# Attention and two MoE layers on one core: TensorE transposes 8 of 18 probability blocks for two of four batches, and the first MoE's small column chain is rewritten

## The chip, the cores and the metric

The kernel runs on one core of a Trainium2 chip. The metric is the device time of one execution in microseconds (us), lower is better. The median of three runs is 1086.21 us (1083.95 to 1088.44). In what follows PE is the matrix engine (TensorE), PEld its weight loads, DVE the VectorE, ACT the ScalarE, POOL the GpSimd engine, and SP the engine whose queue issues nearly all DMA transfers.

## What is computed

```python
def _attn_ref(q, k, v, w1, b1, w2):                 # 4 batches, 8 heads, 576 positions, 64 wide
    scores = scale * np.matmul(q, k.transpose(0, 1, 3, 2)) + bias   # bias from a small MLP of i, j
    attn = np.exp(scores - max) ; attn = attn / (sum(attn) + 1e-9)
    return np.matmul(attn, v)

def _moe_ref(x, w_in, w_out, g_ln):                 # 2304 tokens, 512 -> 1024 -> 512
    h = x @ w_in
    sm = softmax(h) ; solu = h * sm
    ln = (solu - mean(solu)) / np.sqrt(var(solu) + 1e-06) * g_ln
    return ln @ w_out

def _moe2_ref(x, w_gate, w_val, w_out):             # 512 -> 1536 -> 512
    return (sigmoid(x @ w_gate) * (x @ w_val)) @ w_out
```

The attention's output, laid out as 2304 tokens of 512 numbers, goes through the first MoE and then through the second.

## The kernel before

Matrix products are done in f16 with every operand split into a high and a low part: hi is the rounded value, lo the rounded remainder, and a product takes hi x hi, hi x lo and lo x hi.

**Attention** runs as 72 ticks, numbered 0 to 71 here. A tick handles one pair of heads, one batch and 128 queries (for the last 64 positions of a sequence: 64 queries of each of two batches). Ticks 0 to 35 belong to batches 0 and 1, ticks 36 to 71 to batches 2 and 3. In tick t the program writes `a_qk(t)` (scores on PE into the PSUM tiles `s_ps`), `a_soft(t)` (DVE adds the bias and takes the maximum, L550; ACT makes the exponentials, L555 and L557), `a_split(t-1)`, `a_x(t-5)`, some side work, and `a_pv(t-4)` (L590: probabilities times values, into `xps`).

`a_split` makes the f16 parts of the probabilities: hi on ACT (L568) or, in every fourth tick, on DVE (L566); lo on POOL, 1024 columns in L569 and 128 columns in L570. All of it lies in one tile `p16` of 128 x 2304 f16, which is 18 blocks of 128 x 128. One DMA (L572, on SP's queue) transposes all 18 blocks into the tile `pt`, whose blocks are the stationary operands of `a_pv`. The DMA waits for L570, which POOL runs behind L569.

**Side work** is a list of steps, of which five (later three) are taken in each tick: tables for the attention's bias (masks on DVE at L392 and L400, matmuls on PE at L443, sums on DVE at L459 and L463, stores to DRAM as `bias_d`), then decoding and scaling of the first MoE's weights (`w1_steps`, L171 to L180 and L665 to L683), then the first MoE itself (`moe_items`). `scales` in `w1_steps` turns sums of squares into a power of two: a reduction on DVE (L145), one matmul with ones on PE (L147, tile `tot`), and a chain of small DVE operations (L152 to L160, then L689 to L693). `W1S` says how many weight blocks are decoded between the last block of a matrix and its scale.

**The first MoE** takes 18 tiles of 128 tokens. Per tile: `m_g1` (L732, `hps`), `m_ew1` and `m_ew2` (softmax times h and layer norm over 1024 columns, with a chain of operations on 128 x 1 columns of a tile `mm` at L751 to L767, one of them a power on POOL at L765), `m_ew3` (PE transposes the f32 result through the identity `id_sb`, L777 into `ltp`; ACT and DVE copy it out) and `m_g2` (L791, `x2ps`).

**What sets the order.** A scheduler orders the instructions of each engine from priorities and its own estimate of times; each engine then runs its list strictly in that order. From the point where the bias tables are done ("open", about tick 19), PE alone keeps the order in which the code is written. PSUM has two buffers for `s_ps`, one for `xps`, and a ring of three, `ps_m`, that all other PE outputs share: bias matmuls, the transposed q and k (`qtp` L279, `ktp` L240), `xtp`, `hps`, `ltp`, `x2ps`. The ring of `p16` has two buffers and later three, that of `pt` three and later four.

**After attention** the second MoE's weights are decoded and summed (DVE at L172 to L176 and L1188, POOL at L665 and L669) while the first MoE's last tiles finish, and from about 795 us to the end the second MoE's matmuls run on PE.

## Time and profile before

| | us |
|---|---|
| median of three runs | 1086.21 |
| the profiled execution | 1086.11 |
| its span, from the first instruction to the last | 1084.3 |
| 75 to 246 us: attention ticks 0 to 18 with bias tables and the first MoE's weights | 171 |
| 246 to 390 us: ticks 19 to 39 in part, first MoE begins, PE in written order | 144 |
| 390 to 575 us: the other ticks with the first MoE | 185 |
| 575 to 795 us: end of the first MoE, the second MoE's weights | 220 |
| 795 us to the end: second MoE | 289 |

The stretches are set by the starts of ticks: the last PE work of the scheduler's own order stands at about 246 us, the first tick of batches 2 and 3 at 372 us, and the last tick's scores at 563 us. PE is busy for 909.7 us of the span, DVE 776.7, ACT 620.1, POOL 411.1; busy shares are an average over stages with different limits, so the views below are read stage by stage. A wait is shown with the engine that waited, then an arrow, then what ended the wait.

### The profile page before, as it was taken

The numbers are of one execution on the slowest core, as the hardware profiler recorded it, in microseconds if no ns is written. First come the engines' busy times: TensorE is split into PE (matmuls) and PEld (weight loads), VectorE is DVE, ScalarE is ACT, GpSimd is POOL, SyncE is SP. The second block draws the span as 40 slices with busy tenths as digits, with TensorE's granted clock in tenths as the row PEclk, the third lists the DMA queues.
The fourth block names the chain that finished last, engine by engine and source line by source line (L and its number), as shares of the span: only waits on it lengthen the run. The fifth ranks groups of instructions, "written<-read, shape, count | busy, mean of one in ns | idle before, by whom it ended". The sixth has DMA issues, their size and how long they took to land.

```text
span 1084.3 us, 24456 instructions
## 1 busy us (share of the span) xinstructions
PE 909.7 (84%) x9806; PEld 650.8 (60%) x9806; DVE 776.7 (72%) x1605; ACT 620.1 (57%) x1283; POOL 411.1 (38%) x370
## 2 busy tenths in 40 slices
PE   3647584768788889989999788796999999999998
PEld 3534454545565667667776466344577866865873
DVE  6879898985566676666764989999973862881760
ACT  4787676756576788877883677754342331331331
POOL 2357455663555565545561376749000000000000
PEclk9656665779898899999999899998999999999999
DMA  7968999799789899999965536511001010001001
GB/s 229 289 212 217 228 243 266 150 215 225 158 163 188 180 196 189 188 197 204 188 115 165 171 111 193 181 41 39 35 11 54 1 52 27 1 1 39 2 1 39
DMA packets 261442, 146.58 MB, mean 135 GB/s; under 512 B 217680, under 2 KB 231504, under 8 KB 261328
## 3 DMA queue, kind: packets, MB, share of 16 engines
q1 hardware_dynamic: 259264, 143.18, 56.0%
q0 software_dynamic: 1536, 1.58, 0.5%
q8 instruction: 77, 1.26, 0.5%
q14 instruction: 37, 0.30, 0.1%
q10 hardware_dynamic: 528, 0.26, 0.1%
HBM read 82.46 MB, written 20.05 MB: 95 GB/s over the span
## 4 chain that ended last, share of the span: by engine, by line
PE 30%; DVE 14%; DMA 2%; issue 2%; ACT 2%; SPq 0%; POOL 0%; DVEq 0%; ACTq 0%
PE prod L1264 15%; PE ops L1332 10%; DVE fs L1188 4%; DVE w2f L173 2%; DVE w2f L176 2%; PE x2ps L791 2%; PE s_ps L1302 1%; DVE w2s L1188 1%; DVE gv L1170 1%; DMA wraw<-in_moe_w_val_dram 1%; PE hps L732 1%; DVE w2f L172 1%; DMA wraw<-in_moe_w_gate_dram 1%; DVE fr L1308 1%; PE xps L590 1%
## 5 line engine op out<-in xcount | busy, mean ns | idle before, releaser
L569 POOL TENSOR_TENSOR p<-p,p 128x1024 f16<-128x1024 f32 x72 | 155.4, 2159 | 152.1 <-ACT p L568 117.0
L1188 DVE TENSOR_TENSOR fr<-prod,fr 128x512 f32<-128x512 f32 x126 | 85.0, 687 | 93.9 <-PE prod L1264 92.2
L1332 PE MATMUL ops<-w2f,gv 128*128 128x512 f16 x648 | 143.3, 380 | 0.7 <-POOL w2f L669 0.7
L557 ACT ACTIVATE p<-p,m,sc 128x576 f32<-128x576 f32 x144 | 124.0, 862 | 2.8
L550 DVE CUSTOM_DVE_ANT_0 p<-s_ps,gk 128x576 f32<-128x576 f32 x144 | 104.2, 750 | 21.9 <-PE s_ps L530 17.7
L791 PE MATMUL x2ps<-lt,w1f 128*128 128x128 f16 x1728 | 108.0, 223 | 13.6 <-DVE lt L780 12.8
L791 PEld LDWEIGHTS <-w1f 128*128 128x128 f16 x1728 | 102.0, 100 | 22.9 <-issue 18.2
L1302 PE MATMUL s_ps<-xb,w2f 128*128 128x512 f16 (+1 forms) x576 | 101.8, 335 | 16.5 <-DVE fr L1308 13.6
L590 PE MATMUL xps<-gk,pt 128*128 128x64 f16 (+1 forms) x2240 | 90.1, 205 | 29.7 <-DMA pt<-p 25.3
L590 PEld LDWEIGHTS <-pt 128*128 128x128 f16 (+1 forms) x2240 | 84.6, 108 | 40.5 <-DMA pt<-p 27.2
L1332 PEld LDWEIGHTS <-gv 128*128 128x128 f16 x648 | 63.6, 98 | 74.7 <-issue 1.8
L530 PE MATMUL s_ps<-gk,qt 64*128 64x288 f16 (+1 forms) x960 | 93.9, 320 | 10.5 <-DVE m L550 5.3
L443 PEld LDWEIGHTS <-mask 128*128 128x128 f16 (+1 forms) x1312 | 62.6, 119 | 52.6 <-issue 20.7
L1302 PEld LDWEIGHTS <-w2f 128*128 128x128 f16 x576 | 57.6, 100 | 59.2 <-issue 21.5
L1264 PEld LDWEIGHTS <-w2f 128*128 128x128 f16 x864 | 84.5, 98 | 11.8 <-issue 1.1
L1169 ACT ACTIVATE gv<-fr 128x512 f16<-128x512 f32 (+1 forms) x60 | 34.9, 585 | 82.7 <-DVE fr L1322 70.4
L732 PE MATMUL hps<-w1f,xt 128*128 128x512 f16 x312 | 75.7, 392 | 0.6 <-DVE qt L282 0.6
L555 ACT ACTIVATE m<-m,sc 128x1 f32<-128x1 f32 x144 | 40.4, 286 | 54.5 <-DVE m L550 54.5
L443 PE MATMUL bp<-rhs,mask 128*128 128x64 f16 (+1 forms) x960 | 52.2, 222 | 19.8 <-DVE gb L463 12.2
L1264 PEld LDWEIGHTS <-w2s 128*128 128x128 f16 x648 | 63.4, 98 | 7.3
L530 PEld LDWEIGHTS <-qt 64*128 64x128 f16 (+1 forms) x960 | 46.8, 105 | 33.3 <-issue 12.4
L568 ACT ACTIVATE p<-p 128x1152 f16<-128x1152 f32 x54 | 62.6, 1158 | 7.0 <-DMA pt<-p 5.4
(194 smaller groups left out, 1773.3 us busy)
## 6 DMA issues: line engine op xcount, KB each, us to landing
gk<-bias_d SPq DMA_DIRECT2D x24, 576.0 KB
wraw<-in_moe_w_out_dram SPq DMA_DIRECT2D x20, 512.0 KB
wraw<-in_moe_w_gate_dram SPq DMA_DIRECT2D x12, 512.0 KB
wraw<-in_moe_w_val_dram SPq DMA_DIRECT2D x12, 512.0 KB
sraw<-in_q_dram SPq DMA_DIRECT2D x12, 384.0 KB
sraw<-in_k_dram SPq DMA_DIRECT2D x12, 384.0 KB
sraw<-in_v_dram SPq DMA_DIRECT2D x12, 384.0 KB
bias_d<-gk SPq DMA_DIRECT2D x8, 576.0 KB
```

The source lines that it names most:

```text
L443: pe.matmul(big[0:np_, jj // 8, o:o + 64], lhsT, rhs[i].rearrange("p c h g -> p (c h g)"), start=(i == 0), stop=(i == 1),)
L530: pe.matmul(ss[hh][p0:p1, n, 0:288], qt[rows, nr * ql + r, p0:p1], kt[rows, o:o + 288], start=(m == 0), stop=(m == 2))
L550: dve.tensor_tensor_reduce(out=pp[:, hh].rearrange("p (i j) -> p i j", i=2), in0=ss[hh][:, :, 0:288], in1=bi.rearrange("p (i j) -> p i j", ...
L557: act.activation(out=pp[:, hh], in_=pp[:, hh], func=ACTF.Exp, bias=m[:, 2 + hh:3 + hh], scale=col(C), accum_out=sm[:, c + hh:c + hh + 1])
L569: pool.tensor_tensor(out=p16[:, :, 640:1152], in0=pp[:, :, 0:512], in1=hi[:, :, 0:512], op=ALU.subtract)
L590: pe.matmul(o, a, b_, start=(n == 0), stop=(n == len(seq) - 1))
L732: pe.matmul(h, xt[:, xl, kk, off:off + 128], win16[:, 2 * kk + n, wl], start=(kk == 0 and xl == 0 and wl == 0), stop=(kk == 3 and xl == 1),)
L791: pe.matmul(ps[:, dc], wout16[:, f, wl, 128 * dc:128 * dc + 128], lt[:, ll, f], start=(n == 0), stop=(n == 23))
L1188: dve.tensor_tensor(out=out_, in0=a, in1=b, op=op)
L1264: pe.matmul(p[:, jf, 0:nn], w(wl, kk, jf), x(xl, kk), start=(m == 0), stop=(m == 5))
L1302: pe.matmul(ps[:, 0:n], w[:, 4 * (j // 4) + c, wl, o:o + 128], xx[:, 0:n, c, xl, :], start=(m == 0), stop=(m == 11))
L1332: pe.matmul(ps, gvs[j // 4][:, gl, j % 4, 128 * tt:128 * tt + 128], w2h16[2][:, j, wl], start=(m == 0), stop=(m == 35))
```

## The change

For ticks of batches 0 and 1 (`on_pe`), the DMA transposes only the first 10 of the 18 blocks (hi and the 64-column remainders); the other 8 blocks (lo, 512 columns for each of two heads) are transposed by PE against an f16 identity `id16` into a `ps_m` tile `plo`, and ACT copies that tile into the last 8 blocks of `pt` (`a_lo`, written one tick after the split). For this `p16` and `pt` are laid out with the 10 blocks first, POOL does the 128-column operation ahead of the 1024-column one, and the DMA of these ticks waits for the first of the two alone. In ticks of batches 2 and 3 the DMA still moves all 18 blocks and waits for both.

In the first MoE, the column chain loses three DVE operations per tile (two of `m_ew2`'s, between POOL's power and POOL's last pass, and one of `m_ew1`'s); the factor 512 moves into the variance and the multiplication by C1 into the addition before the reciprocal, which takes 1/C1 from a new column. `W1S` goes from 2 to 4, and `scales` is placed behind the scores last written before it.

```diff
-W1S = 2
+W1S = 4
...
     def a_split(i):
         pp = st2.pop(i)
-        p16 = ring("p16", [128, 2, 1152], F16)
-        hi = p16[:, :, 0:576]
+        p16 = ring("p16", [128, 2304], F16)
+        hi = p16[:, 0:1280].rearrange("p (r c) -> p r c", r=2)
+        lo = p16[:, 1280:2304].rearrange("p (r c) -> p r c", r=2)
         if i % 4 in HI_DVE:
-            dve.tensor_copy(hi, pp)
+            dve.tensor_copy(hi[:, :, 0:576], pp)
         else:
-            act.activation(out=hi, in_=pp, func=ACTF.Copy)
-        pool.tensor_tensor(out=p16[:, :, 640:1152], in0=pp[:, :, 0:512], in1=hi[:, :, 0:512], op=ALU.subtract)
-        pool.tensor_tensor(out=p16[:, :, 576:640], in0=pp[:, :, 512:576], in1=hi[:, :, 512:576], op=ALU.subtract)
-        pt = ring("pt", [128, 2, 9, 128], F16)
-        trs[i] = sp.dma_start_transpose(out=pt.rearrange("p r c q -> p (r c) q"), in_=p16.rearrange("p r c -> p (r c)"))
+            act.activation(out=hi[:, :, 0:576], in_=pp, func=ACTF.Copy)
+        pool.tensor_tensor(out=hi[:, :, 576:640], in0=pp[:, :, 512:576], in1=hi[:, :, 512:576], op=ALU.subtract)
+        pool.tensor_tensor(out=lo, in0=pp[:, :, 0:512], in1=hi[:, :, 0:512], op=ALU.subtract)
+        pt = ring("pt", [128, 18, 128], F16)
+        n = 10 if on_pe(i) else 18
+        trs[i] = sp.dma_start_transpose(out=pt[:, 0:n], in_=p16[:, 0:128 * n])
...
+    def on_pe(i):
+        return ticks[i][0] == 0
+
+    def a_lo(i):
+        if i not in los:
+            return
+        lo, pt = los.pop(i), st3[i]
+        ps = ps_m.tile([128, 2, 4, 128], F16, name="plo", tag="m")
+        for hh in range(2):
+            for c in range(4):
+                pe.transpose(ps[:, hh, c], lo[:, hh, 128 * c:128 * c + 128], id16)
+        act.activation(out=pt[:, 10:18], in_=ps.rearrange("p h c q -> p (h c) q"), func=ACTF.Copy)
...
+    def behind(f):
+        with tc.issue_after(glob["qk"].ins):
+            f()
...
-                yield lambda n=n: scales((n - W1S) // 8 - 1)
+                yield lambda n=n: behind(lambda: scales((n - W1S) // 8 - 1))
...
-        dve.tensor_scalar(out=m[:, 3:4], in0=m[:, 2:3], scalar1=1e-9, scalar2=None, op0=ALU.add)
+        dve.tensor_scalar(out=m[:, 3:4], in0=m[:, 2:3], scalar1=1e-9, scalar2=col(RC1), op0=ALU.add, op1=ALU.mult)
         dve.reciprocal(m[:, 3:4], m[:, 3:4])
-        dve.tensor_scalar(out=m[:, 3:4], in0=m[:, 3:4], scalar1=col(C1), scalar2=None, op0=ALU.mult)
...
-        pool.tensor_tensor(out=m[:, 8:9], in0=m[:, 7:8], in1=nhalf, op=ALU.pow)
-        dve.tensor_scalar(out=m[:, 9:10], in0=m[:, 8:9], scalar1=512.0, scalar2=None, op0=ALU.mult)
-        dve.tensor_scalar(out=m[:, 10:11], in0=m[:, 9:10], scalar1=m[:, 5:6], scalar2=None, op0=ALU.mult)
-        pool.tensor_scalar(out=e, in0=e, scalar1=m[:, 9:10], scalar2=m[:, 10:11], op0=ALU.mult, op1=ALU.add)
+        pool.tensor_tensor(out=m[:, 9:10], in0=m[:, 7:8], in1=nhalf, op=ALU.pow)
+        pool.tensor_scalar(out=e, in0=e, scalar1=m[:, 5:6], scalar2=m[:, 9:10], op0=ALU.add, op1=ALU.mult)
...
             if 0 <= t - 1 < nticks:
                 a_split(t - 1)
+            a_lo(t - 2)
```

The order of PE's list, at tick 24. The rows are the scores of tick 24 (`s_ps`), the second half of an `m_g1` step (`hps`), and the transposed keys (`ktp`). Before:

```order
L530 LDWEIGHTS qt
L530 MATMUL s_ps<-gk,qt 128x288
L732 LDWEIGHTS xt
L732 MATMUL hps<-w1f_108,xt 128x512
L732 LDWEIGHTS xt
```

In the changed kernel, from the last of the eight transposes of tick 22 on:

```order
L592 LDWEIGHTS p_4422
L592 MATMUL plo<-id_76,p_4422 128x128
L757 LDWEIGHTS xt
L757 MATMUL hps<-w1f_109,xt 128x512
L757 LDWEIGHTS xt
```

Between the scores and `hps` now stand eight weight loads of lo and eight matmuls. The same holds for each of the 19 groups of tick 17 to tick 35, in a list that is otherwise the same from the scores of tick 19 to the last tick; the 17 groups of ticks 0 to 16 stand in the part that the scheduler orders.

The order of ACT's list, in the same tick: a row of L620 or L640 makes the sums of an earlier tick ready, `xtm` is the copy of a transposed attention output, then come the maxima and exponentials of tick 24. Before:

```order
L620 ACTIVATE sums<-sums 128x8
L653 ACTIVATE xtm<-xtp 128x128
L555 ACTIVATE m<-m,sc 128x1
L557 ACTIVATE p,sums<-p,m,sc 128x576
L555 ACTIVATE m<-m,sc 128x1
```

In the changed kernel:

```order
L640 ACTIVATE sums<-sums 128x8
L673 ACTIVATE xtm<-xtp 128x128
L593 ACTIVATE pt<-plo 128x1024
L556 ACTIVATE m<-m,sc 128x1 x2
L558 ACTIVATE p,sums<-p,m,sc 128x576 x2
```

The copy of the eight blocks stands ahead of the tick's maxima and exponentials.

The order of PE's list at the second `scales`, ahead of the scores of tick 12: `xps` is the product with the values, `qtp` the transposed queries. Before, the `xps` rows that stand here are the last of tick 11:

```order
L590 LDWEIGHTS pt
L590 MATMUL xps<-gk,pt 128x64
L147 MATMUL tot<-acc,ones_sb 128x1
L279 MATMUL qtp<-id_sb,qraw 128x128 x2
L443 LDWEIGHTS mask
```

In the changed kernel they are the tenth of tick 9's 28, and the rest of tick 9 comes behind the scores of tick 12:

```order
L610 LDWEIGHTS pt
L610 MATMUL xps<-gk,pt 128x64
L148 MATMUL tot<-acc,ones_sb 128x1
L280 MATMUL qtp<-id_sb,qraw 128x128 x2
L444 LDWEIGHTS mask
```

So the scores of tick 12 stood behind the products of ticks 10 and 11, and stand now behind ten matmuls of tick 9.

## Rows read from the trace of the kernel before

**Rows 1.** The page: DMA busy share in 40 slices of 27.1 us, and all packets

```profile
DMA  7968999799789899999965536511001010001001
...
DMA packets 261442, 146.58 MB, mean 135 GB/s; under 512 B 217680, under 2 KB 231504, under 8 KB 261328
```

**Rows 2.** Stretches: length, busy us (instructions) of PE, PEld, DVE, ACT, POOL; clock; DMA share, GB/s

```profile
75.00:246.00 171.00, 110.27 (x1444) 81.88 (x1445) 150.85 (x293) 120.30 (x261) 101.72 (x83) 0.64 0.93 214
246.00:390.00 144.00, 118.99 (x1617) 87.46 (x1617) 92.01 (x233) 99.00 (x221) 73.69 (x70) 0.90 0.88 181
390.00:575.00 185.00, 172.09 (x2608) 130.03 (x2605) 122.44 (x342) 149.40 (x331) 102.07 (x84) 0.98 0.96 183
575.00:795.00 220.00, 187.48 (x1419) 112.16 (x1416) 199.97 (x375) 121.40 (x244) 105.19 (x82) 0.96 0.34 111
795.00:1084.00 289.00, 284.71 (x2124) 207.56 (x2122) 155.72 (x251) 81.37 (x132) 0.00 (x0) 1.00 0.06 21
```

**Rows 3.** Waits from 75 to 246 us: who for whom, us in total, times, longest

```profile
PE xps L590 <- DMA pt<-p: 25.3, 6, 10.9
...
DVE cl L152 <- PE tot L147: 4.1, 2, 3.4
```

**Rows 4.** SP's queue in order of time: start, duration, transfer

```profile
125.10 7.02 SPq L572 DMA_TRANSPOSE pt<-p  x2
...
179.72 4.00 SPq L572 DMA_TRANSPOSE pt<-p  x1
```

**Rows 5.** PE in order of time, with the idle time before each row and its releaser

```profile
132.25 1.68 PE L590 MATMUL xps<-gk,pt 128*128 128x64 f16 x28 [10.87 <-DMA pt<-p]
133.74 0.57 PE L147 MATMUL tot<-acc,ones_sb 128*128 128x1 f32 x2
...
181.40 1.68 PE L590 MATMUL xps<-gk,pt 128*128 128x64 f16 x28 [6.15 <-DMA pt<-p]
185.97 1.68 PE L590 MATMUL xps<-gk,pt 128*128 128x64 f16 x28 [2.88 <-DMA pt<-p]
```

**Rows 6.** DVE in order of time, the rows behind its two longest waits of that stretch

```profile
134.35 0.16 DVE L152 TENSOR_SCALAR cl<-tot 128x1 f32<-128x1 f32 x1 [3.44 <-PE tot L147]
...
187.68 0.69 DVE L623 TENSOR_TENSOR xn<-xps,sums 128x512 f32<-128x512 f32 x1 [3.85 <-PE xps L590]
```

**Rows 7.** POOL in order of time, the two operations ahead of a transpose

```profile
121.94 2.14 POOL L569 TENSOR_TENSOR p<-p,p 128x1024 f16<-128x1024 f32 x1
124.02 0.90 POOL L570 TENSOR_TENSOR p<-p,p 128x128 f16<-128x128 f32 x1
```

**Rows 8.** PE in order of time: f16 matmuls of 128 columns, f32 transposes, keys awaited

```profile
297.22 1.51 PE L791 MATMUL x2ps<-lt,w1f 128*128 128x128 f16 x24
...
343.91 1.09 PE L777 MATMUL ltp<-id_sb,e 128*128 128x128 f32 x8
...
373.52 0.84 PE L240 MATMUL ktp<-id_sb,kv 128*128 128x128 f32 x5 [1.80 <-DMA kv<-in_k_dram]
```

**Rows 9.** PE by groups, 246 to 390 us: count, busy us, mean ns, idle before

```profile
L240 PE MATMUL ktp<-id_sb,kv 128*128 128x128 f32 (+1 forms) x40 | 7.1, 280 | 16.5 <-DVE mm L743 3.8 <-DVE mm L759 3.2 <-DVE qt L282 3.2
L777 PE MATMUL ltp<-id_sb,e 128*128 128x128 f32 x32 | 5.9, 319 | 2.9 <-DVE gk L243 1.9 <-DVE qt L282 0.7 <-DVE mm L743 0.2
```

**Rows 10.** ACT by groups, 75 to 390 us

```profile
L568 ACT ACTIVATE p<-p 128x1152 f16<-128x1152 f32 x29 | 33.6, 1158 | 5.8 <-DMA pt<-p 5.4
...
L779 ACT ACTIVATE lt<-ltp 128x512 f16<-128x512 f32 x8 | 4.5, 588 | 0.1
```

**Rows 11.** DVE by groups over the span: the first MoE's small columns

```profile
L767 DVE TENSOR_SCALAR mm<-mm 128x1 f32<-128x1 f32 x18 | 3.8, 210 | 0.4
L756 DVE TENSOR_SCALAR mm<-mm,sc 128x1 f32<-128x1 f32 x18 | 3.7, 208 | 0.2
...
L766 DVE TENSOR_SCALAR mm<-mm 128x1 f32<-128x1 f32 x18 | 2.7, 151 | 9.4 <-POOL mm L765 9.2
```

More of the change, by code (lines that the diff above doesn't have):

```diff
@@ L126, in attn_moe_kernel @@
     id_sb = const.tile([128, 128], F32, name="id_sb")
+    id16 = const.tile([128, 128], F16, name="id16")
     sc = const.tile([128, 32], F32, name="sc")
@@ L132, in attn_moe_kernel @@
     sw = const.tile([128, 3, 16], F32, name="sw")
-    (P_Q, P_K, P_V, P_A, P_W1, P_F, S_Q, S_K, S_V, S_A, S_W1, S_F, C, NC, RB, C1, NC1, CO, RM, RT) = range(20)
+    (P_Q, P_K, P_V, P_A, P_W1, P_F, S_Q, S_K, S_V, S_A, S_W1, S_F, C, NC, RB, C1, NC1, CO, RM, RT, RC1) = range(21)
     (P_G, P_L, P_O, S_G, S_L, S_O, W_CG, W_M) = range(8)
@@ L512, in load_bias @@
         brt[key] = [t[:, hh, :] for hh in range(2)]
-    trs = {}
+    trs, glob = {}, {}
     st1, st2, st3, xps, sums, xns = {}, {}, {}, {}, {}, {}
@@ L529, in a_qk @@
                         o = 640 * kl + 288 * n
-                        pe.matmul(ss[hh][p0:p1, n, 0:288], qt[rows, nr * ql + r, p0:p1], kt[rows, o:o + 288],
-                                  start=(m == 0), stop=(m == 2))
+                        glob["qk"] = pe.matmul(ss[hh][p0:p1, n, 0:288], qt[rows, nr * ql + r, p0:p1], kt[rows, o:o + 288],
+                                               start=(m == 0), stop=(m == 2))
         st1[i] = ss
@@ L562, in a_split @@
         pp = st2.pop(i)
-        p16 = ring("p16", [128, 2, 1152], F16)
-        hi = p16[:, :, 0:576]
+        p16 = ring("p16", [128, 2304], F16)
+        hi = p16[:, 0:1280].rearrange("p (r c) -> p r c", r=2)
+        lo = p16[:, 1280:2304].rearrange("p (r c) -> p r c", r=2)
         if i % 4 in HI_DVE:
-            dve.tensor_copy(hi, pp)
+            dve.tensor_copy(hi[:, :, 0:576], pp)
         else:
-            act.activation(out=hi, in_=pp, func=ACTF.Copy)
-        pool.tensor_tensor(out=p16[:, :, 640:1152], in0=pp[:, :, 0:512], in1=hi[:, :, 0:512], op=ALU.subtract)
-        pool.tensor_tensor(out=p16[:, :, 576:640], in0=pp[:, :, 512:576], in1=hi[:, :, 512:576], op=ALU.subtract)
-        pt = ring("pt", [128, 2, 9, 128], F16)
-        trs[i] = sp.dma_start_transpose(out=pt.rearrange("p r c q -> p (r c) q"), in_=p16.rearrange("p r c -> p (r c)"))
-        st3[i] = pt
+            act.activation(out=hi[:, :, 0:576], in_=pp, func=ACTF.Copy)
[4 more added lines that the diff above has]
+        trs[i] = sp.dma_start_transpose(out=pt[:, 0:n], in_=p16[:, 0:128 * n])
+        st3[i] = pt
+        if on_pe(i):
+            los[i] = lo
+    los = {}
+    def on_pe(i):
[9 more added lines that the diff above has]
+        act.activation(out=pt[:, 10:18], in_=ps.rearrange("p h c q -> p (h c) q"), func=ACTF.Copy)
     def pv_seq(vt, hh, lhs):
@@ L577, in pv_seq @@
         for c in range(5):
-            seq.append((lhs(c), vt[:, hh, c]))
-            seq.append((lhs(c), vt[:, hh, 5 + c]))
+            seq.append((lhs(5 * hh + c), vt[:, hh, c]))
+            seq.append((lhs(5 * hh + c), vt[:, hh, 5 + c]))
         for c in range(4):
-            seq.append((lhs(5 + c), vt[:, hh, c]))
+            seq.append((lhs(10 + 4 * hh + c), vt[:, hh, c]))
         return seq
@@ L596, in a_pv @@
                     po = slice(64 * par, 64 * par + 64)
-                    run(pv_seq(VT[2 * bp + par, hp], hh, lambda c: pt[:, hh, c, po]),
+                    run(pv_seq(VT[2 * bp + par, hp], hh, lambda c: pt[:, c, po]),
                         x[po, 64 * hh:64 * hh + 64])
@@ L606, in a_pv @@
                 o = 256 * bset.index(b) + 128 * r + 64 * hh
-                run(pv_seq(VT[2 * bp + b, hp], hh, lambda c: pt[:, hh, c, :]), x[:, o:o + 64])
+                run(pv_seq(VT[2 * bp + b, hp], hh, lambda c: pt[:, c, :]), x[:, o:o + 64])
     def a_x(i):
@@ L691, in scales @@
                 dve.tensor_scalar(out=col(NC1), in0=col(C1), scalar1=-1.0, scalar2=None, op0=ALU.mult)
+                dve.reciprocal(col(RC1), col(C1))
             else:
@@ L763, in m_ew2 @@
         act.activation(out=mo.pop((i, "hs")), in_=e, func=ACTF.Square, bias=m[:, 5:6], accum_out=m[:, 6:7])
-        dve.tensor_scalar(out=m[:, 7:8], in0=m[:, 6:7], scalar1=1.0 / FF1, scalar2=1e-6, op0=ALU.mult, op1=ALU.add)
-        pool.tensor_tensor(out=m[:, 8:9], in0=m[:, 7:8], in1=nhalf, op=ALU.pow)
-        dve.tensor_scalar(out=m[:, 9:10], in0=m[:, 8:9], scalar1=512.0, scalar2=None, op0=ALU.mult)
-        dve.tensor_scalar(out=m[:, 10:11], in0=m[:, 9:10], scalar1=m[:, 5:6], scalar2=None, op0=ALU.mult)
-        pool.tensor_scalar(out=e, in0=e, scalar1=m[:, 9:10], scalar2=m[:, 10:11], op0=ALU.mult, op1=ALU.add)
+        dve.tensor_scalar(out=m[:, 7:8], in0=m[:, 6:7], scalar1=2.0 ** -18 / FF1, scalar2=1e-6 * 2.0 ** -18,
+                          op0=ALU.mult, op1=ALU.add)
+        pool.tensor_tensor(out=m[:, 9:10], in0=m[:, 7:8], in1=nhalf, op=ALU.pow)
+        pool.tensor_scalar(out=e, in0=e, scalar1=m[:, 5:6], scalar2=m[:, 9:10], op0=ALU.add, op1=ALU.mult)
     def m_ew3(i):
@@ L932, in attn_moe_kernel @@
     sp.dma_start(out=id_sb, in_=ident)
+    pool.tensor_copy(id16, id_sb)
     load_q((0, 0, 0, 0))
@@ L966, in attn_moe_kernel @@
     xn_p = enter(att, "xn", 2, "right")
-    glob = {}
     s1 = ExitStack()
```

## The prediction

> **What bounds the kernel now.** I read the stretches first [rows 2], since the shares over the whole span mix five stages. The last one is plain: from 795 us on PE is busy 284.7 of 289 us, and the change has nothing there. From 390 to 575 us PE is busy 172.1 of 185 us, so PE bounds that stretch too. From 575 to 795 us it is DVE, with 200.0 of 220 us. That leaves two stretches for the transposes. From 75 to 246 us DVE is busy 150.9 of 171 us, so 20.2 us idle is the most that anything which isn't DVE work can give back; the DMA engines are busy for 0.93 of that stretch and the digits of the page are mostly 7 to 9 up to slice 18 [rows 1, 2]. From 246 to 390 us no engine is full: PE 119.0 of 144 us, so 25.0 us idle, ACT 99, DVE 92.
>
> Next come the waits of the first stretch [rows 3]: PE stood still 25.3 us for `pt`, the transposed probabilities, once for 10.9 us. The order of time shows how. SP issues the transposes of ticks 4 and 5 from 125.10 us on [rows 4], and PE starts tick 4's products at 132.25 us after 10.87 us of idle time [rows 5]; tick 11's transpose starts at 179.72 us and its products at 185.97 us. So 18 blocks take 7.2 and 6.3 us from issue to use, 6.7 us in the mean. What PE lost isn't what the kernel lost, though. During the 10.87 us DVE worked on other things from its list, and it ran dry only for 3.44 us, for the matmul `tot` that stood on PE behind tick 4's products [rows 5, 6]. At 187.68 us it waited 3.85 us for tick 11's products. These two waits, 7.3 us together, are what the transposes demonstrably cost DVE.
>
> **The transposes, 75 to 246 us.** Removed are 8 of 18 blocks in 36 of 72 DMAs. If each row of a block (128 x 2 bytes) is one packet, 72 x 18 x 128 = 165,888 of the 217,680 packets under 512 B are transposes [rows 1], and 36 x 8 x 128 = 36,864 of them go (an estimate from the shapes). Cut in the proportion of blocks, 6.7 us becomes 3.7 us, 3.0 us less. The DMA also no longer waits for POOL's 128x1024 operation, 2.14 us, since the 128-column one now comes first and is the one waited for [rows 7]. So ten of the blocks should arrive some 5.1 us earlier in each tick. Both DVE waits are shorter than that, and I count them gone: -7.3 us. The order agrees: scores of tick 12 stood behind the products of ticks 10 and 11 and stand now behind ten matmuls of tick 9. Of the other 12.9 us of DVE's idle time I take a fifth, 2.7 us, because ACT's hi conversion also waited 5.4 us for `pt`'s DMA to give `p16` back [rows 10] and because the other transfers on SP's queue stand behind fewer packets. Together -10 us; what is late next is DVE's own list. The bounds are 0 (another wait takes each place) and -20.2 us (DVE never idle). A loss here I exclude down to a few us: the added work of 17 ticks stays on engines with room, as follows.
>
> **What is added.** Per tick eight f16 matmuls of 128 columns on PE. The nearest row has 24 of them in 1.51 us at full clock, 63 ns each, so 0.50 us for eight; f32 transposes of the same shape, eight in 1.09 us, are the upper bound [rows 8]. ACT's copy of 1024 columns lies between 588 ns for 512 columns out of PSUM and 1158 ns for 1152 columns [rows 10]: 588 + 512 x (1158 - 588) / 640 = 1044 ns, 1.04 us. For 17 ticks that is 17.7 us of ACT on 120.3 of 171 us, and at half clock 17 us of PE on 110.3 of 171 us: both find room.
>
> The Trainium skill's page "TensorE: Matmul & The Clock Gate", section "Part 4: PE-mode transpose", speaks against this change: it gives about 275 ns for a 128x128 transpose within a kernel. By it eight would cost 2.2 us a tick. This case's groups show a mean of 319 ns for one f32 transpose, yet 32 of them in 5.9 us busy, 0.18 us each, because they overlap [rows 9]; so the page's figure fits one instruction's time from end to end here and not its share of PE. The sum would be that of the last rival by the page, and is the one below by the rows.
>
> **The same work from 246 to 390 us.** Here PE keeps the written order, so the eight transposes of ticks 17 to 35 stand between the scores of a tick and the first MoE's steps, 19 groups x 0.50 = 9.5 us. PE is busy 0.83 of that stretch, and I take the same share of the added work as lying on the path: 7.9 us. Less is due to one wait, 1.80 us for keys whose load stands behind transposes [rows 8], which should go: +6.1 us. Low bound: all of it falls into the 25.0 us of idle time, -1.8 us. High bound: the ring of three `ps_m` buffers gets another tenant in every tick. PE already idled 16.5 us ahead of the transposes of keys, 40 matmuls in eight groups of five, mostly for DVE to empty a buffer [rows 9]. If each of the eight groups waits for one ACT copy more, 8 x 1.04 = 8.3 us are added to the full 9.5: +17.8 us. I stay near the middle because the copy is due right after the transposes on an ACT that is busy 99 of 144 us.
>
> **The column chain.** Three small DVE operations per tile go, of 210, 208 and 151 ns, 0.57 us [rows 11], and DVE no longer waits for POOL's power (9.2 us over the span). From 390 to 575 us PE bounds and hides nearly all of that: -1 us (0 to -2). From 575 us on DVE is the bound and some four of 18 tiles are left: 4 x 0.57 = 2.3, so -2 us (0 to -5 where the shorter chain also lets the last tiles end earlier).
>
> **`scales` later and `id16`.** The scale's matmul and its small DVE chain are the same work. The wait of 3.44 us at it is counted above; behind the last scores it can no longer delay those, and DVE's operations queued behind the wait are weight decoding. The f16 copy of the identity is one POOL operation, long before its first use. 0 us, up to 2 us either way if a weight block's split is late for the first MoE.
>
> **The sum.** -10 + 6.1 - 1 - 2 = -6.9 us. The profiled execution took 1086.11 us, 0.1 us below the median of 1086.21, so both give 1079 us.
>
> **Rivals.** *DVE hides the DMA anyway* (also if a transpose's time doesn't follow its blocks): DVE was busy through most of PE's 25.3 us, and its list still holds the weight work between the scores of ticks 11 and 12. Then the first stretch gives 3 us, the second costs 6.1, the chain gives 3: 1086 us. For it speaks that 150.9 of 171 us are DVE work; against it, the two waits that end at transposes. *DMA was the real limit*: with 0.93 busy, every load and store of that stretch gets faster, DVE is never idle, and the second stretch swallows the added matmuls: -20 - 1.8 - 3, 1061 to 1064 us. Against it speaks that such packing was reached nowhere in that stretch. *Slower: the PE list in written order*, ticks 17 to 35. The transposes and their `ps_m` buffer cost the high bound of 17.8 us while the first stretch gives 7.3 and the chain 3: +7.5, 1094 us. It decides from 10.3 us in 19 ticks, 0.54 us per tick; the 16.5 us already lost at the keys speak for it, ACT's free time against. *Transposes that don't overlap*: 8 x 0.319 = 2.55 us per tick, 19 ticks, 0.83 of them on the path, +40 us: 1086 - 13 + 40 = 1113 us; the 5.9 us for 32 speak against it. The page named above stands for this one.
>
> **How the numbers follow.** A measurement of this kernel can tell about 0.5%, 5.4 us, from no change: below 1080.8 is faster, above 1091.6 slower. The forecast (1073 to 1085) has 0.45, hidden DMA 0.24, DMA as the limit 0.13, the written order 0.16, transposes without overlap 0.02. Of the forecast's chance 0.35 lies below 1080.8 and 0.10 above. Faster: 0.35 + 0.13 = 0.48; the same: 0.10 + 0.24 = 0.34; slower: 0.18. The range reaches to the limit case and to the written order, 1063 to 1094 us, which leaves out the last rival and the outer halves of two others.
>
> **What would show it.** Right: PE's wait for `pt` in the first stretch falls from 25.3 us to under 10, DVE's idle time there from 20 to about 10, and PE reaches the written order about 10 us before 246 us; from there to the end of attention some 6 us are given back; `plo` matmuls take about 0.5 us for eight and ACT's copies about 1.04 us. Wrong: DVE idles as long for other things; `ktp`, `hps` or `plo` rows on PE wait for ACT's copy; eight transposes take over 1 us; or DVE's list after 575 us, which the scheduler orders anew, comes out longer by more than the chain saves.

## The result

The changed kernel takes 1092.95 us (median of 16 runs, 1087.45 to 1101.21), the kernel before 1084.79 us (16 runs). The ratio is 1.0071, 95% interval 1.0055 to 1.0088: slower by 0.7%, where 1079 us and a gain were forecast. The profiled execution is the changed kernel's fastest, 1087.45 us with a span of 1085.7 us, so its profile shows only 1.4 us of the loss; a second profile, below, is of a longer run.

The same stretches as in [rows 2], in the changed kernel (length, then busy us and instructions of PE, PEld, DVE, ACT, POOL, the granted clock, the DMA share and GB/s):

```profile
75.00:246.00 171.00, 113.96 (x1594) 88.18 (x1595) 150.67 (x295) 133.56 (x278) 95.60 (x81) 0.67 0.78 192
246.00:390.00 144.00, 121.07 (x1725) 89.68 (x1721) 87.66 (x211) 112.83 (x233) 73.06 (x73) 0.94 0.64 142
390.00:575.00 185.00, 172.70 (x2656) 130.28 (x2654) 121.49 (x322) 152.32 (x339) 99.54 (x84) 0.99 0.97 185
575.00:795.00 220.00, 189.67 (x1390) 113.90 (x1389) 198.96 (x362) 121.54 (x242) 110.94 (x82) 0.94 0.35 111
```

The DMA share fell from 0.93 to 0.78 and from 0.88 to 0.64. But DVE's busy time in the first stretch is what it was, 150.67 of 171 us after 150.85, so DVE stands idle as long as before. ACT has 13 and 14 us more work. The packets on the page of the changed kernel, against [rows 1]:

```profile
DMA packets 224580, 137.17 MB, mean 126 GB/s; under 512 B 180816, under 2 KB 194640, under 8 KB 224464
```

Those under 512 B are 217680 - 180816 = 36,864 fewer, the number worked out from the shapes. SP's queue in order of time, an issue of ten blocks, against [rows 4] where one of 18 took 3.5 to 4.0 us (over the first stretch single issues of ten take 1.3 to 3.7 us, of 18 took 2.7 to 6.4):

```profile
125.16 1.97 SPq L575 DMA_TRANSPOSE pt<-p  x1
```

PE's wait for transposed blocks in the first stretch, 25.3 us in [rows 3], and its longest wait there now, for DVE's sum ahead of `tot` (0.8 us in 75 to 246 us before):

```profile
PE xps L610 <- DMA pt<-p: 2.5, 2, 1.5
PE tot L148 <- DVE acc L146: 12.9, 2, 12.0
```

And DVE's waits there, to be read beside [rows 3] and [rows 6] (who for whom, us in total, times, longest):

```profile
DVE p L551 <- PE s_ps L531: 5.8, 4, 2.5
DVE btmp L460 <- PE bp L444: 4.3, 7, 1.3
DVE w1f L173 <- ACT w1f L172: 4.0, 3, 2.0
DVE acc L146 <- ACT wjunk L707: 2.3, 1, 2.3
DVE cl L153 <- PE tot L148: 1.4, 2, 0.7
DVE xn L643 <- PE xps L610: 0.7, 1, 0.7
```

Both waits that the prediction counted are gone: 3.44 us for `tot` became 0.7 at most, 3.85 us for tick 11's products became 0.7. Others stand in their place, two of them for ACT. What was added, first PE's eight transposes of one tick in order of time, once at a granted clock of 0.50 (119 to 121 us) and once at 1.00 (299 to 301 us), then ACT's copies by groups in 75 to 390 us (count, busy us, mean ns, idle before):

```profile
119.80 1.01 PE L592 MATMUL plo<-id,p 128*128 128x128 f16 x8 [0.54 <-DVE gk L244]
300.03 0.62 PE L592 MATMUL plo<-id,p 128*128 128x128 f16 x8
```

```profile
L593 ACT ACTIVATE pt<-plo 128x1024 f16<-128x1024 f16 x36 | 36.5, 1014 | 15.2 <-PE plo L592 14.9
```

So blocks, transposes and copies are there near the sizes foreseen (0.50 us for eight transposes at full clock, 1.04 us for a copy), and the kernel got slower. Whether the waits went because of the smaller DMAs is taken up below.

### The profile page after: what moved, and what is told of

It is laid out like the page before. It is cut to its first block, busy times and chain, and to the rows that moved or that the text cites. A ratio compares the mean times of both kernels' runs of the same rounds, so it can differ in the third digit from the quotient of the medians.

```text
span 1085.7 us, 25049 instructions
## 1 busy us (share of the span) xinstructions
PE 919.3 (85%) x10094; PEld 662.4 (61%) x10094; DVE 769.7 (71%) x1552; ACT 649.8 (60%) x1319; POOL 408.5 (38%) x371
## 2 busy tenths in 40 slices
DMA packets 224580, 137.17 MB, mean 126 GB/s; under 512 B 180816, under 2 KB 194640, under 8 KB 224464
## 5 line engine op out<-in xcount | busy, mean ns | idle before, releaser
L531 PE MATMUL s_ps<-gk,qt 64*128 64x288 f16 (+1 forms) x960 | 89.2, 314 | 5.5 <-DVE m L551 2.2
L610 PE MATMUL xps<-gk,pt 128*128 128x64 f16 (+1 forms) x2240 | 83.8, 199 | 8.6 <-DVE xn L643 4.8
L571 POOL TENSOR_TENSOR p<-p,p 128x128 f16<-128x128 f32 x72 | 31.8, 442 | 154.0 <-ACT p L570 107.9
L610 PEld LDWEIGHTS <-pt 128*128 128x128 f16 (+1 forms) x2240 | 78.6, 105 | 17.4 <-issue 7.8
L757 PEld LDWEIGHTS <-xt 128*128 128x128 f16 x384 | 37.0, 101 | 46.2 <-issue 11.0
```

Source lines behind the costliest of these rows:

```text
L531: glob["qk"] = pe.matmul(ss[hh][p0:p1, n, 0:288], qt[rows, nr * ql + r, p0:p1], kt[rows, o:o + 288], start=(m == 0), stop=(m == 2))
L610: pe.matmul(o, a, b_, start=(n == 0), stop=(n == len(seq) - 1))
L757: pe.matmul(h, xt[:, xl, kk, off:off + 128], win16[:, 2 * kk + n, wl], start=(kk == 0 and xl == 0 and wl == 0), stop=(kk == 3 and xl == 1),)
```

## Experiments

All ratios are to the kernel before, with runs of both on one chip. Each kernel's lists are ordered anew by the scheduler, and kernels that differ in a trifle came out up to half a per cent apart (0.9898 and 0.9845 below, a copy of one column and one of 128), so smaller differences between two kernels are not put down to an operation. The difference of two ratios carries both intervals: some 2.5 to 4 us either way in what follows. A length of a stretch is from one profile of each kernel.

### Which part of the change

Three causes stood against each other: the transposes on PE with their copies (H1), DVE's list after 575 us with the shorter chain (H2), the later scales (H3).

The transposes, layout and POOL's order alone (the changed kernel with this, and the column chain as before):

```diff
-W1S = 4
+W1S = 2
...
-                yield lambda n=n: behind(lambda: scales((n - W1S) // 8 - 1))
+                yield lambda n=n: scales((n - W1S) // 8 - 1)
```

> The transposes alone (new layout, POOL's order, 8 of 18 blocks on PE in ticks 0 to 35); column chain and scales as before. Theory H1 (the transposes cost what the change lost, by PE's written order in ticks 17 to 35): slower by 0.4 to 0.8%, and by about 5 us more from tick 19 to tick 36. H2 (the stage after 575 us, ordered anew with the shorter chain, lost it): within 0.2% of before. H3 (the later scales lost it): within 0.2% of before.

Measured: 1.0061 (1.0040 to 1.0082).

The column chain alone, in the kernel before:

```diff
+                dve.reciprocal(col(RC1), col(C1))
...
-        dve.tensor_scalar(out=m[:, 9:10], in0=m[:, 8:9], scalar1=512.0, scalar2=None, op0=ALU.mult)
-        dve.tensor_scalar(out=m[:, 10:11], in0=m[:, 9:10], scalar1=m[:, 5:6], scalar2=None, op0=ALU.mult)
...
```

> The shorter column chain alone. H1 and H3: 0 to 0.3% faster, since three small DVE operations per tile go. H2: slower by 0.3 to 0.7%, all of it after 575 us.

Measured: 0.9998 (0.9984 to 1.0012).

The later scales alone, in the kernel before:

```diff
-W1S = 2
+W1S = 4
...
-                yield lambda n=n: scales((n - W1S) // 8 - 1)
+                yield lambda n=n: behind(lambda: scales((n - W1S) // 8 - 1))
```

> W1S = 4 and scales behind the scores, alone. H1 and H2: within 0.2% of before. H3: slower by 0.3 to 0.7%, seen by tick 19.

Measured: 0.9989 (0.9973 to 1.0004).

The changed kernel with PE in no tick, so that all 18 blocks go by DMA:

```diff
     def on_pe(i):
-        return ticks[i][0] == 0
+        return False
```

> The changed kernel with all 18 blocks transposed by DMA in every tick: new layout, POOL's 128-column operation first, chain and scales stay changed. H1: at before's time or up to 0.3% faster. H2 and H3: slower by 0.5 to 0.8%, as the changed kernel.

Measured: 0.9956 (0.9940 to 0.9972). So H1 holds: without the transposes on PE the change is a small gain, with them a loss, 1.0071 - 0.9956 = 1.15% or 12.5 us. Where that small gain is from was asked with layout and POOL's order alone, the same edit with column chain and scales as before:

```diff
-        return ticks[i][0] == 0
+        return False
```

> The kernel before with the new layout of the probabilities and POOL's 128-column operation ahead of the 1024-column one, all 18 blocks by DMA in every tick, column chain and scales as before. If the 0.44% that the kernel with PE in none gained over before come from layout and POOL's order: 0.996 to 0.997. If they come from chain and scales together (0.9998 and 0.9989 alone): 0.999 to 1.000.

Measured: 0.9986 (0.9970 to 1.0002). Layout, chain and scales give 1.5 + 0.2 + 1.2 = 2.9 us of the 4.8 us, each within its error of nothing.

The profile of the later scales alone shows something else: both DVE waits that the prediction put down to the transposes are gone there, with all 18 blocks by DMA. DVE's wait for `tot` is 0.7 us at most, and tick 11's products are not among its waits in the first stretch:

```profile
DVE cl L152 <- PE tot L147: 1.4, 2, 0.7
PE xps L590 <- DMA pt<-p: 16.0, 5, 6.5
```

That kernel is 1.2 us faster, with an error of 1.7. So another order of the lists removes the two waits, and their 7.3 us did not come back to the kernel. PE's wait for blocks is no better a sign: with the same ten blocks it is 11.7, 19.1, 22.0 and 16.6 us in the four kernels below whose products need no copy (nothing added, one column, whole copy unread, copy from SBUF), and 2.5 us in the changed kernel. Here is the one with one column:

```profile
PE xps L610 <- DMA pt<-p: 19.1, 7, 11.9
```

### Early or late ticks

```diff
-        return ticks[i][0] == 0
+        return i < 17
```

> The changed kernel with PE's transposes in ticks 0 to 16 alone, where a scheduler sets PE's order; ticks 17 to 71 move all 18 blocks by DMA. Both ends are known: 1.0071 times the kernel before with PE in ticks 0 to 35, 0.9956 with PE in none. Theory L (PE's written order in ticks 17 to 35 loses the time): 0.9956 or below, since the first stretch has only the gain, and tick 19 starts no later than with PE in none. Theory E (the added work also hurts where the scheduler sets the order, so that the gain never came): 1.000 or more, with tick 19 some 3 us later than with PE in none, as the profiles of the changed kernel and of the one with PE in none stood apart (3.2 us at tick 19, 9.8 us at tick 36).

Measured: 0.9980 (0.9960 to 0.9999).

```diff
-        return ticks[i][0] == 0
+        return 17 <= i < 36
```

> The changed kernel with PE's transposes in ticks 17 to 35 alone, where PE keeps the written order. Theory L: 1.005 or more, some 10 us over the kernel with PE in none (0.9956). The two profiles so far share the loss as 3.2 us up to tick 19 and 6.6 us from there to tick 36: by these 0.9956 + 6.6/1085 = 1.002. Theory E: the larger part came from the first stretch, so 0.998 or less.

Measured: 1.0009 (0.9990 to 1.0028). Over the kernel with PE in none this is 2.6 us for the early ticks, about the error of 2.7 us, and 5.8 us for the late ones: the ticks in written order lose, and for the early ones a loss is not shown. Neither theory's numbers came.

### Relief, PE's work and ACT's copy apart

Ten blocks by DMA and nothing added (`pe_lo` is `on_pe` of the tick):

```diff
-        ps = ps_m.tile([128, 2, 4, 128], F16, name="plo", tag="m")
...
-        act.activation(out=pt[:, 10:18], in_=ps.rearrange("p h c q -> p (h c) q"), func=ACTF.Copy)
...
-            seq.append((lhs(10 + 4 * hh + c), vt[:, hh, c]))
+            seq.append((lhs(5 * hh + c if pe_lo else 10 + 4 * hh + c), vt[:, hh, c]))
```

> The changed kernel without the added work: in ticks 0 to 35 the DMA moves ten blocks, nothing moves the other eight, and the products with the values read the blocks of hi in their place, so the lo part of the probabilities is left out of the result for these two batches. All counts of matmuls with the values stay. It prices the removed DMA work by itself. If the removed blocks are worth the 10 us that the prediction gave them (plus the free matmul slots of the second stretch), 0.9956 - 0.009 = 0.987 or below. If DVE's list hid the transposes anyway (the rival of the prediction), 0.994 to 0.996, and the added work alone, 1.0071 - 0.995 = 1.2%, made the change slower.

Measured: 0.9895 (0.9867 to 0.9922). The removed DMA work is worth 0.9956 - 0.9895 = 0.61%, 6.6 us with an error of 3.4: more than nothing, and the 0.9% expected for the full gain lies at the edge. What was added then costs 1.0071 - 0.9895 = 1.76%, 19 us.

PE's transposes with a copy of one column:

```diff
-        act.activation(out=pt[:, 10:18], in_=ps.rearrange("p h c q -> p (h c) q"), func=ACTF.Copy)
+        act.activation(out=pt[:, 10, 0:1], in_=ps[:, 0, 0, 0:1], func=ACTF.Copy)
```

> The kernel with ten blocks by DMA and PE's eight transposes per tick, but ACT copies only one column (128x1) of the PSUM tile, and the products read the hi blocks in place of the lo ones, so the lo part of the probabilities is left out for two batches. It parts the added work of 1.0071 - 0.9895 = 1.76% (19 us) into PE's and ACT's. Theory P (PE's time counts: 20 x 0.65 us = 13 us in the stretch in written order): 1.000 or more. Theory A (ACT's copy counts, as it stands in ACT's list ahead of the tick's maxima and exponentials and waits there for PE): 0.992 to 0.995, near the kernel without any of the added work (0.9895).

Measured: 0.9898 (0.9873 to 0.9924). PE's transposes, with 36 copies of one column (5.9 us of ACT), cost 0.3 us of those 19, with an error of 4. Theory P, which wanted 13 us, falls; what is left is ACT's copy.

The copy behind the tick's exponentials:

```diff
-            act.activation(out=pp[:, hh], in_=pp[:, hh], func=ACTF.Exp, bias=m[:, 2 + hh:3 + hh], scale=col(C),
+            glob["exp"] = act.activation(out=pp[:, hh], in_=pp[:, hh], func=ACTF.Exp, bias=m[:, 2 + hh:3 + hh], scale=col(C),
...
-        act.activation(out=pt[:, 10:18], in_=ps.rearrange("p h c q -> p (h c) q"), func=ACTF.Copy)
+        with tc.issue_after(glob["exp"].ins):
+            act.activation(out=pt[:, 10:18], in_=ps.rearrange("p h c q -> p (h c) q"), func=ACTF.Copy)
```

> The changed kernel with one difference: ACT's copy of the transposed blocks is placed behind the exponentials of the tick, no longer ahead of the tick's maxima. PE's list and all work stay. Theory A, in the form that the copy's place does it (in the changed kernel's trace ACT waits 9.6 us for PE at the copies between 246 and 390 us): a gain of 6 us or more on the changed kernel, 1.0015 or below, and ticks 19 to 36 take 122 to 124 us, where they took 128.3. If it is the copy's duration that counts (20 x 1.02 us) and not its place: within 0.3% of the changed kernel. Theory P: no gain.

Measured: 1.0217 (1.0189 to 1.0246), 15 us slower than the changed kernel. The place ahead of the maxima was not the fault; a later copy is worse, so with the same copies their place moves the time by 15 us. Why it is so much worse was not taken apart.

The copies of ticks 17 to 35 on DVE:

```diff
-        act.activation(out=pt[:, 10:18], in_=ps.rearrange("p h c q -> p (h c) q"), func=ACTF.Copy)
+        if i < 17:
+            act.activation(out=pt[:, 10:18], in_=ps.rearrange("p h c q -> p (h c) q"), func=ACTF.Copy)
+        else:
+            dve.tensor_copy(pt[:, 10:18], ps.rearrange("p h c q -> p (h c) q"))
```

> The changed kernel with the copies of ticks 17 to 35 on DVE, which is busy 88 of 144 us there, in place of ACT (113 of 144). Theory A: ACT's 20 us of copies go, DVE has room: 1.000 or below. Theory P: within 0.3% of the changed kernel's 1.0071. If DVE's list carries the path of that stretch (bias and maxima stand there): above 1.0071.

Measured: 1.0039 (1.0022 to 1.0055), against 1.0083 for the changed kernel on that chip. DVE is no free place either.

The changed kernel again:

> The changed kernel once more, beside the others on the same chip, and with a second profile, since the first profile is of its fastest run (1087.45 us, the median is 1092.95). 1.007 again by the sixteen runs before. If the profile is of a run near the median, ticks 0 to 36 should show where the other 5 us are: by the kernel with the transposes alone (its profile: 3.2 us later at tick 19 and 8.9 us at tick 36 than before) in the stretch in written order.

Measured: 1.0083 (1.0055 to 1.0112); the profile has a span of 1097.2 us. It starts tick 19 at 249.1 us (before 248.9) and tick 36 at 380.1 us (372.5), and loses 4.0 us more by tick 71, where the first profile had won 3.7 back.

### What of the copy costs

One block copied, and read in the place of all eight:

```diff
-        act.activation(out=pt[:, 10:18], in_=ps.rearrange("p h c q -> p (h c) q"), func=ACTF.Copy)
+        act.activation(out=pt[:, 10], in_=ps[:, 0, 0], func=ACTF.Copy)
...
-            seq.append((lhs(10 + 4 * hh + c), vt[:, hh, c]))
+            seq.append((lhs(10 if pe_lo else 10 + 4 * hh + c), vt[:, hh, c]))
```

> Ten blocks by DMA, PE's eight transposes per tick, and ACT copies one of the eight blocks (128 columns), which the products with the values read in the place of all eight: so the lo part of the probabilities is replaced by wrong blocks for two batches. The products still wait for the copy, which takes some 0.27 us (the row of 128 columns on ACT) in place of 1.02 us. Duration theory: 0.9898 + 36 x 0.27 us / 36 x 1.02 us of 1.8% = 0.994 at most. Wait theory (the products wait for POOL, PE and ACT in a row): 1.004 or more.

Measured: 0.9845 (0.9825 to 0.9865). The products wait for POOL, PE and ACT in a row as in the changed kernel, and it is the fastest of all. The wait theory falls.

The whole copy, with nobody waiting for it:

```diff
-            seq.append((lhs(10 + 4 * hh + c), vt[:, hh, c]))
+            seq.append((lhs(5 * hh + c if pe_lo else 10 + 4 * hh + c), vt[:, hh, c]))
```

> The changed kernel with its whole copy of eight blocks on ACT, but the products read the blocks of hi in place of lo, so they wait for no copy; the lo part is left out for two batches. Duration theory, and the theory that the copy holds the shared PSUM buffer: 1.004 or more, near the changed kernel's 1.0071 to 1.0083. Wait theory: 0.992 or less, near the kernel with the one-column copy (0.9898).

Measured: 1.0129 (1.0099 to 1.0160). So the loss is there although no product waits for the copy. That it is larger than the changed kernel's is not explained: its profile has 186.7 us up to tick 19, where the changed kernel's two have 175.6 and 176.9, and 131.1 us from there to tick 36, as they have.

One column copied, and besides a copy of the same length from SBUF:

```diff
-        act.activation(out=pt[:, 10:18], in_=ps.rearrange("p h c q -> p (h c) q"), func=ACTF.Copy)
+        act.activation(out=pt[:, 10, 0:1], in_=ps[:, 0, 0, 0:1], func=ACTF.Copy)
+        act.activation(out=pt[:, 10:18], in_=lo.rearrange("p h (c q) -> p (h c) q", q=128), func=ACTF.Copy)
...
-            seq.append((lhs(10 + 4 * hh + c), vt[:, hh, c]))
+            seq.append((lhs(5 * hh + c if pe_lo else 10 + 4 * hh + c), vt[:, hh, c]))
```

> The kernel with PE's transposes and the one-column copy (0.9898), and in addition ACT copies the eight blocks of lo untransposed, from SBUF to SBUF, behind the one-column copy, and nobody reads that (the lo part is left out for two batches). ACT has the copy's time, but the copy neither holds a PSUM buffer nor waits for PE. Duration theory: 1.003 or more. If holding the PSUM buffer for 1 us longer, or the wait on PE, is what costs: 0.990 to 0.993.

Measured: 1.0129 (1.0101 to 1.0156). The long copy holds no PSUM buffer, reads nothing of PE's and no product waits for it, and it costs 0.0129 + 0.0102 = 2.3%, 25 us over the one-column kernel (0.9898), for 36 x 1.05 = 38 us of ACT. It reads `p16` and so holds that buffer instead, which the copy out of PSUM does not. What the two expensive copies have in common is their time in ACT's list: that is the cause, in ticks with room on ACT by its busy share.

Half the blocks:

```diff
-        n = 10 if on_pe(i) else 18
+        n = 14 if on_pe(i) else 18
...
-        act.activation(out=pt[:, 10:18], in_=ps.rearrange("p h c q -> p (h c) q"), func=ACTF.Copy)
+        act.activation(out=pt[:, 14:18], in_=ps, func=ACTF.Copy)
```

> The changed kernel with 14 blocks by DMA, and PE and ACT moving only the four of one head (copy of 512 columns; 588 ns for such a row). Duration theory: the relief halves (0.61% to 0.3%) and the copy's price goes with 588 of 1018 ns (1.76% to 1.0%): 0.9956 - 0.003 + 0.010 = 1.003. Wait theory: the wait keeps its length, the relief halves: 1.007 or more.

Measured: 1.0017 (0.9993 to 1.0042), as the duration theory has it.

How that works is read from ticks 19 to 36, from the start of tick 19's bias sum on DVE to that of tick 36: the same work in every kernel. The rows are of the view of stretches; before, the kernel with ten blocks and nothing added, the one with PE's transposes and one column, the changed kernel's second profile, and the one with the copy from SBUF:

```profile
248.90:372.50 123.60, 100.37 (x1301) 71.33 (x1301) 79.67 (x201) 85.58 (x188) 62.10 (x58) 0.90 0.90 179
```

```profile
246.50:362.10 115.60, 94.41 (x1306) 67.74 (x1306) 78.75 (x188) 85.01 (x189) 60.49 (x61) 0.97 0.67 153
```

```profile
244.40:366.00 121.60, 102.74 (x1450) 75.40 (x1449) 77.70 (x186) 87.97 (x208) 63.93 (x63) 0.97 0.67 152
```

```profile
249.10:380.10 131.00, 106.42 (x1447) 77.40 (x1445) 78.38 (x187) 99.78 (x205) 60.47 (x61) 0.93 0.63 138
```

```profile
249.50:390.40 140.90, 111.78 (x1446) 80.73 (x1447) 78.54 (x188) 104.78 (x224) 65.46 (x64) 0.88 0.59 129
```

The columns to read are the length (second number) and ACT's busy time (the fourth with a count). The difference is ACT's idle time:

| kernel | length | ACT busy | ACT idle |
|---|---|---|---|
| before | 123.6 | 85.6 | 38.0 |
| PE in none | 121.5 | 84.8 | 36.7 |
| ten blocks, nothing added | 115.6 | 85.0 | 30.6 |
| PE's transposes, one column | 121.6 | 88.0 | 33.6 |
| one block | 121.8 | 88.7 | 33.1 |
| half the blocks | 130.7 | 94.5 | 36.2 |
| changed, first profile | 128.3 | 99.8 | 28.5 |
| changed, second profile | 131.0 | 99.8 | 31.2 |
| whole copy, nobody waits | 131.1 | 99.8 | 31.3 |
| whole copy, late ticks alone | 129.6 | 100.0 | 29.6 |
| whole copy behind the exponentials | 146.2 | 101.8 | 44.4 |
| one column and copy from SBUF | 140.9 | 104.8 | 36.1 |
| short copy (next section) | 127.5 | 94.7 | 32.8 |
| short copy, late ticks alone (next section) | 122.9 | 92.7 | 30.2 |

But for the copy behind the exponentials, ACT's idle time stays between 28 and 38 us while its work grows from 85 to 105 us: little of the added work goes into it, and the stretch gets longer. (Not by ACT alone: kernels with 93 to 95 us of ACT differ by 8 us.) ACT idles in short waits within each tick, for DVE's maximum and for PE; before, and in the changed kernel's first profile, 246 to 390 us:

```profile
ACT m L555 <- DVE m L550: 25.3, 13, 4.9
```

```profile
ACT pt L593 <- PE plo L592: 9.6, 9, 3.0
ACT m L556 <- DVE m L551: 7.5, 7, 2.4
```

Its own results are waited for in turn. That a copy put into its list delays the next exponential by most of its length is the reading that fits; no view of single ticks was taken to show it. The rows show a second part that goes with it. For the same 1446 to 1450 matmuls PE is busy 102.7 us at a granted clock of 0.97 with one column copied, 106.4 at 0.93 in the changed kernel and 111.8 at 0.88 with the copy from SBUF, and its idle time between them grows too, from 18.9 to 29.1 us. Of the 19.3 us between the first and the last of these lengths, 9.0 are PE's own matmuls taking longer; the relief has the same part, with PE busy 100.4 us at 0.90 before and 94.4 at 0.97 with ten blocks and nothing added. What the clock costs apart from the waits was not measured.

With the late copies on DVE, ACT has 86.5 us of work, but DVE 87.1, and the length is the changed kernel's:

```profile
250.70:380.10 129.40, 108.57 (x1449) 79.43 (x1447) 87.12 (x206) 86.53 (x189) 63.70 (x61) 0.92 0.62 141
```

### A shorter copy of all the blocks

```diff
-        act.activation(out=pt[:, 10:18], in_=ps.rearrange("p h c q -> p (h c) q"), func=ACTF.Copy)
+        act.activation(out=pt[:, 10:18].rearrange("p n q -> p (n q)").bitcast(F32), in_=ps.rearrange("p h c q -> p (h c q)").bitcast(F32), func=ACTF.Copy)
```

> The changed kernel with one difference: ACT copies the transposed blocks as 512 columns of f32, each a pair of neighbouring f16, in place of 1024 columns of f16. A row of 512 columns of f32 out of PSUM took 588 ns, the copy now takes 1018. Duration theory: 36 x 0.43 us = 15.5 us of ACT's time go, and at the price found between copies of 128 and of 1024 columns ((1.0071 - 0.9845) x 1085 us / (36 x 0.75 us) = 0.9 us per us) the changed kernel's 1.0071 to 1.0083 become 0.994 to 0.996. If the copy costs by something other than its time: within 0.4% of the changed kernel.

Measured: 1079.34 us, 0.9926 (0.9898 to 0.9954), 1.5% under the changed kernel and the only version with every block transposed that beats the kernel before by over 0.5%. Against the kernel with PE in none (0.9956) the gain is 3.3 us with an error of 3.5, so that PE's transposes pay even so is not shown. Its copies in 75 to 390 us:

```profile
L593 ACT ACTIVATE pt<-plo 128x512 f32<-128x512 f32 x36 | 21.2, 590 | 19.1 <-PE plo L592 18.9
```

36.5 - 21.2 = 15.3 us of ACT are gone, and (1.0077 - 0.9926) x 1085 = 16.4 us of the kernel's time, with 1.0077 as the mean of the changed kernel's two ratios. In its profile the ticks up to 19 take 167.0 us, where they took 176.9 before and 175.6 in the changed kernel. The rows of the view of stretches for that, of the changed kernel and of this one:

```profile
71.90:247.50 175.60, 115.46 (x1634) 89.38 (x1635) 153.16 (x305) 136.22 (x282) 99.21 (x86) 0.67 0.78 192
```

```profile
72.00:239.00 167.00, 109.47 (x1635) 85.68 (x1636) 149.37 (x304) 128.80 (x282) 98.33 (x84) 0.71 0.83 201
```

ACT has 7.4 us less to do there and the stretch is 8.6 us shorter. That is not ACT's work alone: the kernels with ten blocks and nothing or little added have less of it there, 123 to 125 us, and take 169.9 to 173.7 us. (Whether every pair of f16 passes an f32 copy with its bits unchanged, above all pairs that read as subnormal f32, was not measured.)

The same copy, in the late ticks alone:

```diff
-        return ticks[i][0] == 0
+        return 17 <= i < 36
```

> The same, with PE's transposes and the shortened copies in ticks 17 to 35 alone, and all 18 blocks by DMA in ticks 0 to 16. With the copy of 1024 columns there the ratio was 1.0009. Duration theory: 19 x 0.43 x 0.9 = 7.4 us less, 0.994. Against the first kernel of this job: where the first stretch gains nothing from fewer blocks (by the profiles it starts tick 19 no earlier), leaving out its 17 x 0.59 us of copies should make this the faster of the two, 0.990 to 0.994.

Measured: 0.9958 (0.9932 to 0.9985). It beats the same ticks with the long copy (1.0009) by 5.5 us of the 7.4 expected, and from tick 19 to 36 the stretch goes from 129.6 to 122.9 us with 7.3 us less of ACT's work. That it would beat the kernel with short copies in all 36 ticks did not come: it is 3.5 us slower, within the error of 4.2, so a gain of the early ticks isn't shown either.

## Why the prediction was wrong

**The step that failed** is in "What is added": the copies, 17.7 us on 120.3 of 171 us of ACT, "find room", and on an ACT "busy 99 of 144 us" they have free time. They were costed at nothing. They cost 1.0071 - 0.9898 = 1.7%, 19 us for 36.5 - 5.9 = 30.6 us more of copies: the busy share said that ACT had room, but its idle time is made of short waits inside a tick. No row of before shows directly what an added microsecond on ACT costs; the bounds should have run from 0 to the copies' full 36.5 us.

**The first stretch, -10 us.** By the two profiles tick 19 starts 1.4 us earlier and 0.2 us later than before. The first signs came, but not by the mechanism: both DVE waits went, and they went too with the later scales alone and all 18 blocks by DMA, for 1.2 us of the kernel's time, and PE's wait for blocks, 2.5 us here, is 19.1 us with the same ten blocks and a copy of one column. So the second step that failed is the -7.3 us: the two waits were counted as the transposes' price, and DVE idled for other things instead. (A fifth of 12.9 us is 2.6, not 2.7.) With short copies the ticks up to 19 are 176.9 - 167.0 = 9.9 us shorter than before, with long ones 1.3 or none, so the long copies may have taken a gain away. In the kernels with ten blocks and nothing or little added this stretch takes 173.7, 171.6 and 169.9 us, where the one with PE in none takes 172.4; so how much of it is relief and how much the new order of the lists stays open.

**The stretch in written order, +6.1 us.** Tick 19 to 36 became 4.7 and 7.4 us longer, near the forecast by luck. PE's transposes with one-column copies lengthen it from 115.6 to 121.6 us: 6.0 us for the 7.9, in their place. In the same two profiles tick 19 starts 2.1 us earlier and 1.9 us come back behind tick 36, so that little is left over the whole kernel (0.3 us by the ratios); and orders alone make nearly the same work here differ by 4.6 us (127.5 and 122.9 with the short copies). The 1.8 us for relief are 5.9 (121.5 to 115.6 us), and layout, chain and scales give 2.1 more. The copies on ACT, at 0, cost 6.7 and 9.4 us (121.6 to 128.3 and 131.0). Two wrong terms, relief and copies, nearly cancelled.

**The column chain, -3 us.** Alone it gives 0.2 us, with an interval of -1.7 to +1.3 us. The 0.57 us of DVE per tile after 575 us do not show in the time. **The scales, 0 us:** -1.2, within the 2 us given.

**The rivals.** The slower one gave the right side and nearly the time, 1094 us, but by another mechanism: the `ps_m` ring and PE's list. PE's list with eight transposes more per tick costs nothing measurable over the whole kernel, and the loss appears too when the long copy holds no PSUM buffer. "DVE hides the DMA" is half right: removing the DMA work alone is worth 6.6 us (error 3.4), where 10 + 1.8 were forecast. Transposes that don't overlap are out: eight take 0.62 us at full clock and 1.01 us at half. The groups here have a mean of 228 to 256 ns for one instruction from end to end, and 0.62 / 8 = 78 ns is its share in a row of eight. The Trainium skill's page "TensorE: Matmul & The Clock Gate", section "Part 4: PE-mode transpose", gives some 275 ns for one; the trace comes near it for one instruction, and not for the time that a row of them takes.

**What would show it.** The line for "wrong" that said "DVE idles as long for other things" is what the profile shows: 20.3 us after 20.2. The 10 us at 246 us did not come. PE's wait for `pt` fell to under 10 us as the line for "right" had it, which by the kernels above is no sign of the smaller DMA.

## What to carry over

A busy share tells how much an engine has to do, not what an added instruction costs: where engines hand work to each other several times per tick, an engine that is 70% busy can still pass on more than half of every microsecond that it is given (19 of 30.6 us here, 25 of 38), so price an addition on each engine that it touches between nothing and its full length. To tell which, give the engine a copy that nobody reads. When a wait disappears, that is not yet a gain, and no proof that the operation blamed for it caused it: look at a kernel in which that operation stays as it was. And when data only has to be moved, move it in fewer, wider elements.

## What the hardware showed

The copy on ACT goes by the number of columns, not by bytes: 1024 f16 took 1014 ns, 512 f16 590 ns, 512 f32 590 ns, 128 f16 268 ns, one column 165 ns. The Trainium skill's page "ScalarE: Activation LUTs", section "Step-by-step: what each stage is for", states one element per cycle and lane, for fp32 and bf16 alike; the two rows of 512 columns, f32 and f16, agree. Here are the copies of 512 f16 columns (half the blocks) and of 128 (one block):

```profile
L592 ACT ACTIVATE pt<-plo 128x512 f16<-128x512 f16 x36 | 21.2, 590 | 17.9 <-PE plo L591 17.8
```

```profile
L593 ACT ACTIVATE pt<-plo 128x128 f16<-128x128 f16 x36 | 9.6, 268 | 25.1 <-PE plo L592 25.0
```

The price of a microsecond on ACT isn't the same throughout: from no copies to 21.2 us of them the ratio went from 0.9895 to 0.9926, 3.4 us with an error of 4.2, and by the next 15.3 us it rose by 16.4 us. Nor is it the same for the same copies' time: the kernel with half the blocks has 21.2 us too, and if its relief is half of 0.61% (an estimate, 0.9925 without copies), they cost it 10 us. Where the step lies, and why, was not settled.
